# A fused attention and gated-MLP kernel: batch 1's first block set ahead of batch 0's token mixing, token weights and attention 2 placed elsewhere, and k loaded without zeros

## The chip, the cores and the metric

The kernel runs on one core of a Trainium2 chip. Its time is the device time of one execution in microseconds (us), the median of several runs. Before the change it is 541.98 us (three runs, 540.46 to 542.31). The core's engines are TensorE (PE, matmuls, with PEld for its weight loads), VectorE (DVE), ScalarE (ACT), GpSimd (POOL) and SyncE (SP, which here only issues DMA transfers). Each takes its instructions in the order in which the program lists them.

## The reference

There are four batches of 576 positions. A masked attention of 8 heads comes first, then a gated MLP that mixes positions, then a second block that mixes positions again:

```python
scores = where(mask, q @ k.T / sqrt(64), -1e9)   # heads 0-3: the last 32 keys; heads 4-7: earlier keys, same position mod 32
x = softmax(scores) @ v                          # (4, 576, 512) after the heads are put side by side
h = relu(x @ w_in); u, v = h[..., :512], h[..., 512:]
v_n = (v - mean(v)) / sqrt(var(v) + 1e-6)
x = (u * (w_spatial @ v_n + b_spatial)) @ w_out
theta = x @ w_theta
y = w_tok_r @ (x * cos(theta)) + w_tok_i @ (x * sin(theta))
z = x + y
out = z + relu(z @ w_ch)
```

## The kernel before

Nearly all matmuls use pairs of 16-bit numbers (a high part and the rest) with three passes for each product, so each operand is split once by ACT (high part) and by DVE or POOL (low part). The weights arrive as 64-bit words and are converted on the way: a part of a weight is loaded into a staging buffer, `from_f64` (L196) makes 32-bit numbers of it with one ACT and three DVE instructions, and `part` (L209) splits it with one ACT and one POOL instruction. The token weights `wtok` (for `w_tok_r` and `w_tok_i`) come in nine such parts, `wch` (for `w_ch`) in four.

For each batch b the PE's main work goes through these steps, named here as in the trace: **v** (`main_v`: x times the half of `w_in` that is normalized; its result `vn` comes from DVE, ACT and POOL), **u** and **sp** (`main_mid`: the other half of `w_in`, and the first mixing of positions, which reads `vn`; the order is u0, u1, u2, sp0, u3, sp1, sp2, sp3), **x** (times `w_out`), **th** (times `w_theta`, after which cosine and sine and two DMA transposes per quarter fill `zz`), **y** (the token mixing, which reads `zz` and `wtok`) and **c** (times `w_ch`, and out). The steps of one batch follow each other, except that v of the next batch stands between th and y: v covers the time in which `zz` is filled.

Attention runs beside that. It has eleven units (two blocks of two heads) per batch. Batches 0 and 1 use 32-bit numbers (`attention32`), batches 2 and 3 pairs of 16-bit ones (`attention`). A unit is: scores on PE, maximum and exponential, division by the sum (`softmax_div`), a transpose, the product with v, and `x_evac`, which writes the result to `xT` of its batch on ACT and DVE. In `attention32` the mask is added by PE (a matmul with an identity, L383), and the maximum is a DVE reduction (L395). Its k is laid out with zeros, so that one product of 128 rows serves one head of a pair: half of each k load is zeros from memory.

The order of the side work is set by a clock that counts the columns of the main matmuls (`clock`, in us at 2400 columns per us): attention b does a step when the clock passes `ATT_AT[b]` (first step, distance), and a weight part is put in when the clock passes its due time less a lead less a distance for each part after it (`CONV_...`: due, lead, distance). The five constants and the main loop are:

```python
ATT_AT = (None, (2.7, 4.0), (74.5, 4.4), (169.9, 4.6))
CONV_TOK = (61.0, 10.0, 2.0)
...
for b in range(B):
    run_main(main_mid(b))
    end = main_end(b)
    if b + 1 < B:
        drain(b + 1)
        run_main(main_v(b + 1))
    run_main(end)
```

`main_mid` holds u, sp, x and th here, `main_end` y and c. A scheduler then orders each engine's instructions by priority and by its own estimate of when operands are ready.

Of the kernel before, what the change touches and what calls it, by code (L numbers as in the profile page):

```python
# [19 lines left out]
STRIDE = 32  # L20
# [14 lines left out]
E_WAY = ('aaaadaaadaa', 'aaaaaaaaaaa')  # L35
# [18 lines left out]
ATT_AT = (None, (2.7, 4.0), (74.5, 4.4), (169.9, 4.6))  # L54
WIN_AT = (0, 0, 0, 0, 1, 1, 1, 1)
# [3 lines left out]
CONV_TOK = (61.0, 10.0, 2.0)  # L59
CONV_CH = (87.0, 14.1, 2.4)  # L60
# [4 lines left out]
def kernel(  # L65
# [68 lines left out]
    nc.gpsimd.tensor_copy(identb, ident)  # L134
# [166 lines left out]

    def load32(b, hp):
        local = hp < 2
        nb = 6 if local else 5
        qv = att_p.tile([P, S], F32, tag="qT", name="q32", bufs=2)
        kv = att_p.tile([P, 2, S + STRIDE], F32, tag="kT", name="k32", bufs=2)
        ksrc = kzl[b, hp] if local else kzs[b, hp - 2]
        first = b == 0 and hp == 0
        cuts = (0, 2 * LQ, S) if first else (0, S)
        for i, (c0, c1) in enumerate(zip(cuts, cuts[1:])):  # L310
            nc.sync.dma_start(qv[:, c0:c1], qp[b, hp][:, c0:c1])
            k0, k1 = (c0 + STRIDE if i else 0, c1 + STRIDE) if local else (c0, c1)
            nc.sync.dma_start(kv[..., k0:k1], ksrc[..., k0:k1])
            if first and i == 0:
                nc.sync.dma_start(mask, mask_d)
                nc.scalar.activation(maskb, mask, AF.Copy)
        vv = att_p.tile([P, 6, 2, 64], F32, tag="vT", name="v32", bufs=2)
# [21 lines left out]

# [35 lines left out]
    def scores32(u, tabs, sc, apart):  # L375


        R = LQ if units[u][0][0] < 2 else P
        mi = [mask_of(*un) for un in units[u]]
        for j0, j1 in ((0, 1), (1, 2)) if apart else ((0, 2),):  # L380
            for i0, i1 in [(0, 2)] if mi[0] == mi[1] else [(0, 1), (1, 2)]:
                shape = [P, i1 - i0, j1 - j0, P]
                nc.tensor.matmul(sc[0:R, i0:i1, j0:j1], identb[:, 0:R],  # L383
                                 maskb[:, mi[i0], :].unsqueeze(1).unsqueeze(1).broadcast_to(shape),
                                 start=(i0 == 0), stop=False)
        for n, (hp, j, blk) in enumerate(blocks_of(u)):
            o = LQ * blk if hp < 2 else SOFF[blk]
            nc.tensor.matmul(sc[0:R, n // 2, j], tabs[hp][0][:, o:o + R], tabs[hp][1][:, j, o:o + P],
                             start=False, stop=(n == 3 or (apart and n == 2)))
        return R  # L390

    def softmax32(sc, sm, st, R, way):
        X = mybir.AxisListType.X
        mx = st[0:R, 0, :]
        nc.vector.tensor_reduce(out=mx.rearrange("p (i j) -> p i j", i=2), in_=sc[0:R], op=ALU.max, axis=X)  # L395
        smv = sm[0:R].rearrange("p (i j) k -> p i j k", i=2)
        if way == "d":
            nc.vector.tensor_tensor(smv, sc[0:R], mx.rearrange("p (i j) -> p i j", i=2).unsqueeze(3).broadcast_to(
                [R, 2, 2, P]), ALU.subtract)
            nc.scalar.activation(sm[0:R], sm[0:R], AF.Exp, scale=0.125)  # L400
            nc.vector.tensor_reduce(out=st[0:R, 2, :], in_=sm[0:R], op=ALU.add, axis=X)
        else:
            nc.vector.tensor_scalar(st[0:R, 1, :], mx, -0.125, None, op0=ALU.mult)
            for n in range(4):
                nc.scalar.activation(sm[0:R, n, :], sc[0:R, n // 2, n % 2, :], AF.Exp, bias=st[0:R, 1, n:n + 1],
# [488 lines left out]
```

## Time and profile before

| what | us |
|---|---|
| median of three runs | 541.98 |
| the profiled execution's own time | 538.83 |
| its span in the trace | 536.8 |
| PE busy in the span | 485.4 |
| DVE busy | 366.2 |
| ACT busy | 306.9 |
| POOL busy | 96.1 |

The span is the stretch that the trace shows; 2.03 us of the profiled execution lie around it. A row of a timeline begins with start and duration in us, then engine, line of the kernel, operation and operands (out<-in), then shape and count, and in brackets the idle time just before and what ended it. A row of a group has after its bar the busy time in us, the mean duration of one in ns, and the idle time before them with its releasers.

### The profile page before, as it was taken

Reading aid. Unit: us, or ns where it says so; the run is one execution under the profiler, and the core shown is the slowest. Engines: PE = TensorE matmul, PEld = TensorE weight load, DVE = VectorE, ACT = ScalarE, POOL = GpSimd, SP = SyncE. Lnnn points to the kernel's source line nnn. Section 1 sums busy time; section 2 is a strip of 40 time slices with the busy share of each in tenths; the row PEclk is TensorE's granted clock in tenths of the full one; section 3 lists DMA queues with packets and bytes.
Section 4 is the critical chain, followed back from the end, with each engine's and each line's share of the span. In section 5 each row is a group of like instructions: output and inputs, shape, how many; then the busy total and the mean of one; then the engine's idle time right before and its main releaser. Section 6 shows DMA issues by size and latency. Waiting matters only on the chain. (4 is left out here: it accounts for less than half of the span.)

```text
span 536.8 us, 10338 instructions
## 1 busy us (share of the span) xinstructions
PE 485.4 (90%) x4019; PEld 365.7 (68%) x4019; DVE 366.2 (68%) x817; ACT 306.9 (57%) x737; POOL 96.1 (18%) x72
## 2 busy tenths in 40 slices
PE   6777978777887998999899998999999999996996
PEld 6764556555653776777666876777747777774775
DVE  1788999999987998898558778874389121227212
ACT  1777787667798436777585457764582121158101
POOL 0021134543300542001000400010003300100110
PEclk9789999999898998999999999999999999998999
DMA  8666577454159514755529034522082020004402
GB/s 278 239 232 189 162 262 219 161 152 139 37 98 244 136 40 108 194 135 143 137 40 137 1 81 127 148 45 37 1 150 27 1 89 1 1 2 91 86 1 88
DMA packets 75861, 59.88 MB, mean 112 GB/s; under 512 B 59939, under 2 KB 60963, under 8 KB 75813
## 3 DMA queue, kind: packets, MB, share of 16 engines
q1 hardware_dynamic: 75812, 59.23, 42.2%
q8 instruction: 31, 0.51, 0.4%
q14 instruction: 18, 0.14, 0.1%
HBM read 40.08 MB, written 4.72 MB: 83 GB/s over the span
## 5 line engine op out<-in xcount | busy, mean ns | idle before, releaser
L517 PE MATMUL y<-wtok,zf 128*128 128x288 f16 x864 | 108.8, 288 | 4.1 <-DMA zf<-vn 4.1
L517 PEld LDWEIGHTS <-zf 128*128 128x128 f16 x864 | 84.6, 99 | 27.7 <-DMA zf<-vn 4.7
L517 PE MATMUL sp<-wsp,vn 128*128 128x288 f16 x384 | 50.8, 286 | 2.1 <-ACT vn L108 1.6
L517 PE MATMUL c<-x2h,wch 128*128 128x288 f16 x384 | 49.6, 289 | 1.6 <-ACT o L108 1.6
L517 PE MATMUL x<-zf,wout 128*128 128x288 f16 x384 | 49.7, 288 | 0.0
L517 PE MATMUL th<-x2h,wth 128*128 128x288 f16 x384 | 49.6, 290 | 0.0
L517 PE MATMUL u<-xT,win 128*128 128x288 f16 x384 | 49.5, 286 | 0.0
L517 PEld LDWEIGHTS <-vn 128*128 128x128 f16 x416 | 40.3, 98 | 12.3 <-ACT vn L108 1.8
L578 PE MATMUL v<-win,xT 128*128 128x512 f16 x192 | 44.9, 387 | 3.0 <-DVE xT L356 1.9
L108 POOL TENSOR_TENSOR x2h<-x2f,x2h 128x576 f16<-128x576 f32 x20 | 27.6, 1381 | 110.4 <-DVE x2h L108 42.5
L517 PEld LDWEIGHTS <-wch 128*128 128x128 f16 x384 | 37.8, 99 | 11.7 <-issue 2.0
L517 PEld LDWEIGHTS <-wth 128*128 128x128 f16 x384 | 38.1, 100 | 10.3 <-issue 0.2
L517 PEld LDWEIGHTS <-wout 128*128 128x128 f16 x384 | 37.2, 98 | 9.5
L517 PEld LDWEIGHTS <-win 128*128 128x128 f16 x384 | 37.2, 98 | 9.1
L336 ACT ACTIVATE sm<-sm,st 96x128 f32<-96x128 f32 (+1 forms) x88 | 34.2, 390 | 7.8 <-DVE st L332 7.7
L578 PEld LDWEIGHTS <-xT 128*128 128x128 f16 x192 | 18.8, 99 | 25.3 <-DVE xT L356 2.6
L108 ACT ACTIVATE x2h<-x2f 128x576 f16<-128x576 f32 x24 | 16.5, 686 | 30.4 <-DVE x2f L108 30.0
L108 DVE SCALAR_TENSOR_TENSOR x2f<-y,x2f 128x576 f32<-128x576 f32 x16 | 12.0, 752 | 28.5 <-PE y L517 28.5
L108 POOL TENSOR_TENSOR zf<-u,zf 128x576 f16<-128x576 f32 x8 | 10.3, 1287 | 106.5 <-ACT zf L108 106.5
L108 DVE TENSOR_TENSOR ta<-ta,x2f 128x1152 f32<-128x1152 f32 x16 | 21.5, 1352 | 8.9 <-ACT ta L108 8.9
L108 ACT ACTIVATE o<-c 128x576 f32<-128x576 f32 (+1 forms) x17 | 10.3, 613 | 30.3 <-PE c L517 30.0
L343 DVE TENSOR_TENSOR sm<-sm,st 96x512 f32<-96x512 f32 (+1 forms) x33 | 26.7, 809 | 0.8
(122 smaller groups left out, 890.2 us busy)
## 6 DMA issues: line engine op xcount, KB each, us to landing
qs<-in_qd_dram SPq DMA_DIRECT2D x16, 288.0 KB, 3.0
out_dram<-o SPq DMA_DIRECT2D x15, 288.0 KB, 2.1
x2f<-in_w_in_dram SPq DMA_DIRECT2D x8, 512.0 KB, 5.3
ks<-in_kl_dram SPq DMA_DIRECT2D x8, 304.0 KB, 3.1
k<-in_kzs_dram SPq DMA_DIRECT2D x4, 576.0 KB, 5.4
wstg<-in_w_tr_dram SPq DMA_DIRECT2D x4, 576.0 KB, 4.7
wstg<-in_w_ti_dram SPq DMA_DIRECT2D x4, 576.0 KB, 4.7
ks<-in_ks_dram SPq DMA_DIRECT2D x8, 288.0 KB, 3.2
```

The costliest lines, as they stand in the source:

```text
L108: return f(*args, **kwargs)
L336: nc.scalar.activation(sm[0:R, n, :], sm[0:R, n, :], AF.Exp, bias=st[0:R, 1, n:n + 1], scale=-1.0, accum_out=st[0:R, 2, n:n + 1])
L343: N[eng].tensor_tensor(sm[0:R], sm[0:R], st[0:R, 3, :].unsqueeze(2).broadcast_to([R, 4, P]), ALU.mult)
L517: nc.tensor.matmul(ps, lhs, rhs, **kw)
L578: nc.tensor.matmul(ps, xh[:, xe, c, i * P:(i + 1) * P], win[:, we, c, DM:2 * DM], start=(c == 0 and n == 0), stop=(c == NC - 1 and n == 2))
```

## The change

1. The main loop: `main_mid` is cut in two (`main_mid` with u, sp, x, and `main_th` with th). Batch 1's v, u, sp and x now stand ahead of batch 0's y and c; batch 1's th follows c. From v of batch 2 on the order is that of before.
2. Since batch 1's x is made while batch 0's is still needed, batch 1 uses memory that is free then: its gated product lies in `wch`'s place (`gs`), x in that of `xT[0]` and of `vn`, its z in that of `x2h`. Batch 2's attention writes `xT[1]`, batch 3's `xT[0]` (`XAT`).
3. Times of the side work: the nine token parts go from clock 35 to 51 to clock 48.8 to 80, `wch` from 65.7 to 72.9 to 112.5 to 123, attention 2 starts at 63.0 with steps of 5.6 (74.5 with 4.4), attention 3 at 188.5 with 4.0 (169.9 with 4.6). Parts of `w_in` go in from step 3 of attention 0 on, seven of them by step 9 (four by step 7).
4. Attention 0 and 1 are separate functions. In attention 0 the mask is added and the maximum taken in one DVE instruction per block (`softmax_exp`, four per unit), as in attention 2; PE adds no mask there. Its division is on POOL (`softmax_div("g", ...)`, it was "v"); one unit also subtracts on POOL (way "p").
5. k of batches 0 and 1 lies in two fixed tiles, `kts`, whose zero halves are written once by four DVE memsets; each load brings the two non-zero quarters as two DMAs of 64 partitions. The first k loads are issued by ACT.

```diff
-ATT_AT = (None, (2.7, 4.0), (74.5, 4.4), (169.9, 4.6))
-WIN_AT = (0, 0, 0, 0, 1, 1, 1, 1)
+ATT_AT = (None, (2.7, 4.0), (63.0, 5.6), (188.5, 4.0))
+WIN_AT = (0, 0, 0, 1, 1, 1, 1, 1, 1, 1)
...
-CONV_TOK = (61.0, 10.0, 2.0)
-CONV_CH = (87.0, 14.1, 2.4)
+CONV_TOK = (107.0, 27.0, 3.9)
+CONV_CH = (133.0, 10.0, 3.5)
...
+    for t in kts:
+        nc.vector.memset(t[0:64, 1, :], 0.0)
+        nc.vector.memset(t[64:P, 0, :], 0.0)
...
+    gs = [wchf[:, i * S:(i + 1) * S] for i in range(7)] + [gx]
+    x2f1 = xT[0].rearrange("p e c n -> p (e c n)").bitcast(F32).rearrange("p (c n) -> p c n", c=NC)
...
+    XAT = (0, 1, 1, 0)
...
+    def load_kq(qv, kv, b, hp, c0, c1, k0, k1, by=nc.sync):
+        nc.sync.dma_start(qv[:, c0:c1], qp[b, hp][:, c0:c1])
+        ksrc = kzl[b, hp] if hp < 2 else kzs[b, hp - 2]
+        for j in range(2):
+            by.dma_start(kv[64 * j:64 * j + 64, j, k0:k1], ksrc[64 * j:64 * j + 64, j, k0:k1])
...
+                for n, (hp, j, blk) in enumerate(blocks_of(s)):
+                    o = LQ * blk if local else SOFF[blk]
+                    nc.tensor.matmul(scs[n][0:R], tabs[hp][0][:, o:o + R], tabs[hp][1][:, j, o:o + P],
+                                     start=True, stop=True)
+                st = att_p.tile([P, 4, 4], F32, tag="st", name="st", bufs=4)
+                softmax_exp(s, scs, sm, st, E_SUM[s])
...
+                softmax_div("g", sm, st, R, XS)
...
     run_main(main_v(0))
-    for b in range(B):
-        run_main(main_mid(b))
-        end = main_end(b)
+    run_main(main_mid(0))
+    run_main(main_th(0))
+    drain(1)
+    run_main(main_v(1))
+    run_main(main_mid(1))
+    run_main(main_end(0))
+    for b in range(1, B):
+        if b > 1:
+            run_main(main_mid(b))
+        run_main(main_th(b))
         if b + 1 < B:
             drain(b + 1)
             run_main(main_v(b + 1))
-        run_main(end)
+        run_main(main_end(b))
```

**First place: ACT at the start of attention 0.** Before, the first conversion of `w_in` (L203, in `from_f64`) stands ahead of the first exponentials (L405):

```order
1 L316 ACT_TABLE_LOAD
2 L316 ACTIVATE maskb<-mask 128x512
3 L203 ACTIVATE x2f<-x2f 128x512
4 L405 ACTIVATE smx,st<-at,st 96x128 x8
5 L119 ACTIVATE win<-x2h 128x512
```

Now the exponentials are L378 and the conversion is L232; L479 copies a transpose, L420 writes `xT`:

```order
3 L119 ACT_TABLE_LOAD
4 L119 ACTIVATE maskb<-mask 128x512
5 L378 ACTIVATE smx,st<-smx,st 96x128 x9
6 L479 ACTIVATE smx<-sc 128x4x96
7 L378 ACTIVATE smx,st<-smx,st 96x128 x2
8 L420 ACTIVATE xT_101<-av 128x192
9 L378 ACTIVATE smx,st<-smx,st 96x128
10 L479 ACTIVATE smx<-sc 128x4x96
11 L232 ACTIVATE x2f<-x2f 128x512
```

The conversion has gone behind twelve exponentials (three units).

**Second place: PE where v of batch 1 ends.** Before, y of batch 0 follows it (v_1744 is batch 1's last piece of v):

```order
1224 L517 LDWEIGHTS xT_96
1225 L517 MATMUL v_1744<-win,xT_96 64x512
1226 L517 LDWEIGHTS xT_96
1227 L517 MATMUL v_1744<-win,xT_96 64x512
1228 L517 LDWEIGHTS zf
1229 L517 MATMUL y_1800<-wtok,zf 128x288
```

Now u of batch 1 follows:

```order
1150 L587 LDWEIGHTS xT_102
1151 L587 MATMUL v_1716<-win,xT_102 64x512
1152 L587 LDWEIGHTS xT_102
1153 L587 MATMUL v_1716<-win,xT_102 64x512
1154 L587 LDWEIGHTS win
1155 L587 MATMUL u_1763<-xT_102,win 128x288
```

and after u0, u1 and u2 (72 matmuls), 16 score matmuls and 12 of the product with v of attention 2, the first use of batch 1's `vn`, with u3 behind it:

```order
1353 L551 MATMUL av<-pT,areg 64x96
1354 L587 LDWEIGHTS vn
1355 L587 MATMUL sp_1888<-wsp,vn 128x288
1356 L587 LDWEIGHTS vn
1357 L587 MATMUL sp_1888<-wsp,vn 128x288
1358 L587 LDWEIGHTS win
1359 L587 MATMUL u_1963<-xT_102,win 128x288
```

Between v and sp of batch 1 stood y and c of batch 0 and three u; now three u stand there.

**Third place: the token parts on DVE.** Before, after the last gated product of batch 0 (u_967 with sp's result, then zf), token parts (L204, L205, L206 on `wx`) are mixed with attention 1 (st, sc):

```order
204 L108 TENSOR_TENSOR zf<-u_967,zf 128x576
205 L395 TENSOR_REDUCE st<-sc 128x4
206 L204 TENSOR_SCALAR wx<-wstg 128x576
207 L403 TENSOR_SCALAR st<-st 128x4
208 L204 TENSOR_SCALAR wx<-wstg 128x576
209 L205 SCALAR_TENSOR_TENSOR wx<-wstg,wx 128x576 x2
210 L206 SCALAR_TENSOR_TENSOR wx<-wstg,wx 128x576 x2
```

At the same place there is now attention 2's first k (L319) in their stead:

```order
260 L108 TENSOR_TENSOR zf<-u_970,zf 128x576
261 L398 TENSOR_REDUCE st<-sc 128x4
262 L319 TENSOR_TENSOR kt_78<-areg,kt_78 128x608
263 L400 TENSOR_SCALAR st<-st 128x4
264 L406 TENSOR_SCALAR st<-st 128x4
```

One token part (of nine) still stands ahead of the end of th of batch 0; the other eight begin after its first cosine and sine work (ta):

```order
297 L108 SCALAR_TENSOR_TENSOR ta_1482<-th_1413,ta_1482 128x576
298 L108 SCALAR_TENSOR_TENSOR ta_1508<-th_1414,ta_1508 128x576
299 L233 TENSOR_SCALAR wx<-wstg 128x576
300 L108 TENSOR_TENSOR ta_1482<-ta_1482,x2f 128x1152
301 L108 SCALAR_TENSOR_TENSOR ta_1544<-th_1519,ta_1544 128x576
302 L108 TENSOR_TENSOR vn<-ta_1482,vn 128x1152
303 L108 TENSOR_TENSOR ta_1508<-ta_1508,x2f 128x1152
304 L234 SCALAR_TENSOR_TENSOR wx<-wstg,wx 128x576
```

Eight parts have moved from ahead of th's evacuation to behind it; two q and two k preparations of attention 2 have moved the other way.

## Rows read from the trace of the kernel before

**Rows 1.** Busy time of each engine in seven stretches: length, then busy us (instructions) of PE, PEld, DVE, ACT, POOL, then the granted TensorE clock, the DMA engines' share and GB/s. The cuts are: the first conversion of `w_in` begins on ACT and DVE (14.1), the first statistics of v of batch 0 begin (59.5), the first cosine and sine work of batch 0 begins on DVE (146.6), v of batch 1 ends (173.4), c of batch 0 begins (201.9), the first cosine and sine work of batch 1 begins on DVE (271).

```profile
0.00:14.10 14.10, 8.73 (x44) 8.26 (x45) 1.60 (x6) 1.91 (x2) 0.99 (x7) 1.00 0.82 277
14.10:59.50 45.40, 36.63 (x273) 26.36 (x273) 38.74 (x98) 34.24 (x123) 9.10 (x7) 0.89 0.67 220
59.50:146.60 87.10, 70.17 (x575) 52.98 (x572) 84.55 (x160) 63.67 (x167) 33.96 (x23) 0.98 0.50 157
146.60:173.40 26.80, 22.02 (x141) 11.88 (x141) 21.62 (x44) 24.98 (x48) 1.28 (x1) 0.94 0.79 165
173.40:201.90 28.50, 27.89 (x246) 22.39 (x246) 27.42 (x60) 12.15 (x20) 13.76 (x9) 1.00 0.34 96
201.90:271.00 69.10, 64.99 (x629) 50.80 (x628) 53.73 (x148) 47.33 (x135) 6.31 (x5) 0.98 0.56 139
271.00:536.80 265.80, 255.02 (x2124) 193.03 (x2122) 138.56 (x305) 122.64 (x248) 30.71 (x22) 0.99 0.28 58
```

**Rows 2.** The timelines of ACT, of DVE and of PE in the first 62 us, around the first exponentials; the last row is the warm-up, six matmuls of the identity.

```profile
14.12 0.67 ACT L203 ACTIVATE x2f<-x2f 128x512 f32<-128x512 f32 x1 [8.14 <-DMA x2f<-in_w_in_dram]
14.72 0.36 ACT L405 ACTIVATE smx<-at,st 96x128 f32<-96x128 f32 x1
...
1.08 0.48 DVE L149 MEMSET k<- 64x512 f16 x1
...
8.42 0.69 DVE L395 TENSOR_REDUCE st<-at 96x4 f32<-96x512 f32 x1 [6.54 <-PE at L388]
14.12 0.43 DVE L204 TENSOR_SCALAR x2h<-x2f 128x512 int32<-128x512 int32 x1 [5.02 <-DMA x2f<-in_w_in_dram]
...
1.36 2.93 PE L794 MATMUL av<-ident 128*128 128x128 f32 x12 [1.36 <-POOL ident masks.py:199]
```

**Rows 3.** Groups of instructions by line and shape, whole span: the parts of an attention unit on DVE (the reduction; the division; in attention 2 and 3 the masked maximum and the read of its accumulator), POOL's split of a token part and of a `w_in` part, and one shape of the mask matmuls of attention 0 on PE.

```profile
L395 DVE TENSOR_REDUCE st<-at 96x4 f32<-96x512 f32 x6 | 4.1, 684 | 8.7 <-PE at L388 8.7
L343 DVE TENSOR_TENSOR smx<-smx,st 96x512 f32<-96x512 f32 x6 | 4.5, 751 | 0.0
L332 DVE CUSTOM_DVE_ANT_0 sm<-sc,mask 96x128 f32<-96x128 f32 x48 | 11.1, 280 | 0.0
L332 DVE DVE_READ_ACCUMULATOR2_ANT st<- 96x1 f32 x48 | 3.8, 78 | 0.0
L211 POOL TENSOR_TENSOR wtok<-wx,wtok 128x576 f16<-128x576 f32 x9 | 13.6, 1520 | 23.2 <-ACT wtok L119 16.7 <-DVE x2h L108 6.5
L211 POOL TENSOR_TENSOR win<-x2h,win 128x512 f16<-128x512 f32 x8 | 10.3, 1296 | 48.7 <-ACT win L119 48.7
...
L383 PE MATMUL at<-maskb,identb 128*128 128x256 bf16 x10 | 2.3, 301 | 0.8 <-ACT smx L405 0.8
```

**Rows 4.** Durations in ns (least, median, greatest) of two lines of DVE, then the timeline of DVE and of POOL around one of the long ones.

```profile
L332 DVE CUSTOM_DVE_ANT_0 sm<-sc,mask x88: 271/282/292, 159.4 to 361.7; 96x128 f32<-96x128 f32 x48, 128x128 f32<-128x128 f32 x40
...
L341 DVE TENSOR_SCALAR st<-st x44: 134/167/2099, 16.4 to 363.0; 96x4 f32<-96x4 f32 x24, 128x4 f32<-128x4 f32 x20
...
80.57 2.10 DVE L341 TENSOR_SCALAR st<-st 96x4 f32<-96x4 f32 x1
...
78.10 4.54 POOL L108 TENSOR_TENSOR vn<-vr,vn 128x1024 f16<-128x1024 f32 x1 [1.65 <-ACT vn L108]
```

**Rows 5.** Groups of DVE in the stretch 59.5 to 146.6: the nine token parts, and attention 2's q and k.

```profile
L206 DVE SCALAR_TENSOR_TENSOR wx<-wstg,wx 128x576 int32<-128x576 int32 x9 | 7.7, 865 | 0.0
L205 DVE SCALAR_TENSOR_TENSOR wx<-wstg,wx 128x576 int32<-128x576 int32 x9 | 7.6, 852 | 0.0
...
L204 DVE TENSOR_SCALAR wx<-wstg 128x576 int32<-128x576 int32 x9 | 5.0, 565 | 1.1 <-POOL wtok L211 1.1
...
L288 DVE TENSOR_TENSOR qT<-qs,qT 64x576 f16<-64x576 f32 x2 | 2.6, 1284 | 0.1
...
L290 DVE TENSOR_TENSOR kT<-ks,kT 128x608 f16<-128x608 f32 x2 | 1.6, 784 | 0.0
```

**Rows 6.** What PE waited for in the stretch 59.5 to 146.6: us in total, times, longest. L445 is attention 1's transpose.

```profile
PE av L445 <- DVE xT L356: 7.7, 5, 3.1
PE av L445 <- DVE sm L343: 5.9, 3, 2.5
PE sp L517 <- ACT vn L108: 1.6, 1, 1.6
```

**Rows 7.** Timelines of PE, DVE and POOL: the end of v and the making of `vn`, of batch 1 (first three rows) and of batch 2 (next three); then the scores of one unit of attention 2 and one u of batch 1.

```profile
172.62 0.83 PE L517 MATMUL v<-win,xT 128*64 128x512 f16 x5
...
193.26 1.94 DVE L108 TENSOR_TENSOR vn<-vr,vn 64x512 f16<-64x512 f32 x2
...
194.29 2.90 POOL L108 TENSOR_TENSOR vn<-vr,vn 128x1024 f16<-128x1024 f32 x1 [1.25 <-ACT vn L108]
...
287.12 1.49 PE L517 MATMUL v<-win,xT 128*64 128x512 f16 x12
...
300.35 1.22 DVE L108 TENSOR_TENSOR vn<-vr,vn 128x1024 f16<-128x1024 f32 x1
...
300.35 3.20 POOL L108 TENSOR_TENSOR vn<-vr,vn 128x1024 f16<-128x1024 f32 x1 [1.25 <-ACT vn L108]
...
223.03 0.62 PE L458 MATMUL sc<-kT,qT 128*128 128x128 f16 x8
223.49 3.10 PE L517 MATMUL u<-xT,win 128*128 128x288 f16 x24
```

More of the change, by code (lines that the diff above doesn't have):

```diff
@@ L310, in load32 @@
         for i, (c0, c1) in enumerate(zip(cuts, cuts[1:])):
-            nc.sync.dma_start(qv[:, c0:c1], qp[b, hp][:, c0:c1])
             k0, k1 = (c0 + STRIDE if i else 0, c1 + STRIDE) if local else (c0, c1)
[L313 to L317, printed above, removed]
+            load_kq(qv, kv, b, hp, c0, c1, k0, k1, nc.scalar if first else nc.sync)
+            if first:
+                nc.sync.dma_start(mask[:, 2 * i:2 * i + 2], mask_d[:, 2 * i:2 * i + 2])
+        nb = 6 if local else 5
         nc.sync.dma_start(vv[:, 0:nb], vl_d[b, hp] if local else vs_d[b, hp - 2])
@@ new lines, in softmax_exp @@
+        if way == "p":
+            nc.gpsimd.tensor_tensor(sm[0:R], sm[0:R], st[0:R, 0, :].unsqueeze(2).broadcast_to([R, 4, P]), ALU.subtract)
+            nc.scalar.activation(sm[0:R], sm[0:R], AF.Exp, scale=0.125)
+            nc.vector.tensor_reduce(out=st[0:R, 2, :], in_=sm[0:R], op=ALU.add, axis=mybir.AxisListType.X)
+        else:
+            for n in range(4):
+                nc.scalar.activation(sm[0:R, n, :], sm[0:R, n, :], AF.Exp, bias=st[0:R, 1, n:n + 1],
+                                     scale=-1.0, accum_out=st[0:R, 2, n:n + 1])
@@ new lines, in softmax_exp, with scores32 @@
+        return R
+    def scores32(u, tabs, sc):
+        R = LQ if units[u][0][0] < 2 else P
+        mi = [mask_of(*un) for un in units[u]]
+        for i0, i1 in [(0, 2)] if mi[0] == mi[1] else [(0, 1), (1, 2)]:
+            nc.tensor.matmul(sc[0:R, i0:i1], identb[:, 0:R],
+                             maskb[:, mi[i0], :].unsqueeze(1).unsqueeze(1).broadcast_to([P, i1 - i0, 2, P]),
+                             start=(i0 == 0), stop=False)
+        for n, (hp, j, blk) in enumerate(blocks_of(u)):
+            o = LQ * blk if hp < 2 else SOFF[blk]
+            nc.tensor.matmul(sc[0:R, n // 2, j], tabs[hp][0][:, o:o + R], tabs[hp][1][:, j, o:o + P],
+                             start=False, stop=(n == 3))
+        return R
@@ L373, in spans_of @@
         return spans
[L375 to L405, printed above, removed]
-                                     scale=0.125, accum_out=st[0:R, 2, n:n + 1])
@@ L411, in attention32, with attention1 @@
+    def attention1():
+        b = 1
+        tabs = {0: load32(b, 0)}
+        copy(N, "v", identb, ident)
+        copy(N, "a", maskb, mask)
         yield
@@ L763 @@
     timed(sq_parts(wch, w_ch), *CONV_CH)
-    atts = [(attention32 if b < N32 else attention)(b) for b in range(B)]
+    atts = [attention0(), attention1()] + [attention(b) for b in range(N32, B)]
     att = {"b": 1, "n": 0}
```

148 lines of the change are left out of this document (100 added, 48 removed).

## The prediction, made before the changed kernel ran

> **What bounds the kernel now.** I read the busy time by stretch first [rows 1]. In the last stretch, from 271 us on, PE is busy 255.0 of 265.8 us: there PE alone decides, and the change leaves the order of that work as it is. Half the span is therefore outside the change. In the first 271 us three stages behave differently. Up to 14.1 us hardly anything but transfers runs (DVE busy 1.6 us). From 59.5 to 146.6 us, which is u, sp, x and the beginning of th of batch 0, DVE is busy 84.55 of 87.1 us and PE 70.17: DVE is the bound. From 146.6 to 271 us PE is busy 22.02 + 27.89 + 64.99 = 114.9 of 124.4 us and DVE 21.62 + 27.42 + 53.73 = 102.8: PE is nearly the bound, with 9.5 us of gaps.
>
> Then the waits of PE in the stage where DVE is the bound [rows 6]: 7.7 and 5.9 us for DVE's last step of a unit of attention 1 or its division. DVE comes late because other work, the weight parts above all [rows 5], stands ahead in its queue.
>
> Last the start [rows 2]. DVE has the first maximum at 8.42 + 0.69 = 9.11 us, but the first exponential (L405) begins at 14.72: ACT sat for 8.14 us in front of a conversion of `w_in` whose transfer had not landed, and the exponentials are queued behind it.
>
> **The change, part by part.** The sum is made against the profiled execution, 538.83 us (span 536.8 and 2.03 around it); the median of the runs shown is 541.98, which is 3.15 more.
>
> *The start, up to 59.5 us.* The conversion now stands behind twelve exponentials on ACT and likewise further down on DVE. So the wait from 9.11 to 14.72 goes: 5.6 us. What is late next is the chain of the unit itself, in which three things change. The reduction (0.684) and the division (0.751) leave DVE, four masked maxima (4 x 0.280, or 4 x 0.358 if the read of the accumulator counts in full) come [rows 3]: per unit between 0 and 0.3 us less, for eleven units 0 to 3.5 us less. The division goes to POOL, where a `w_in` split of nearly the same size takes 1.296 [rows 3]. POOL is free (9.1 of 45.4 us busy, rows 1), but a long POOL instruction can hold up DVE: a DVE tensor_scalar of 0.167 us (median) took 2.10 us, from 80.57 to 82.67, while POOL ran from 78.10 to 82.64 [rows 4]. Eleven divisions cost DVE between nothing and 11 x 1.3 = 14 us that way. The masked maximum is not hit so in the rows (292 ns at most, rows 4), and most of the unit's DVE time is masked maxima now, so I take a fifth of it, 3 us. Four memsets come ahead of the first maximum; a memset of 64x512 16-bit numbers took 0.48 [rows 2], these have 608 32-bit numbers, so 0.5 to 1.2 us each, 2 to 4.6 us in all. They run while the first q, k and mask are still on the way, and the first maximum began only at 8.42, so I take nothing; without that cover up to 4.6 would be lost. The mask matmuls that go (ten of 301 ns are shown, rows 3) and the warm-up, now behind the first scores (2.93 us, rows 2), lie on PE, which idles 8.8 of 45.4 us there; I count both at nothing, and 2.9 us if the warm-up is in the way of the first transposes. Half of k's bytes go; with DMA at 0.67 of its time [rows 1] that can only bring `w_in` sooner, and I count it at nothing too. Together: -5.6 + 3 = -2.6, call it -3, with ends of -9 (no hold-up, all of the DVE saving) and +9 (all 14 us of it).
>
> [...]
>
> *From 59.5 to 146.6 us.* Eight of nine token parts leave it. On DVE a part is 0.865 + 0.852 + 0.565 = 2.28 us [rows 5], some 0.2 less back to back, so 8 x 2.07 = 16.6 us go. Two q and two k of attention 2 come, at the means of other such instructions 2 x 1.284 + 2 x 0.784 = 4.1 [rows 5], of which the q's mean holds a hold-up, so 3.4. DVE's 84.55 becomes 71.4. PE keeps its 70.17. POOL loses eight splits of 1.520 [rows 3], 12.2 of its 33.96 us, and with them some hold-ups. Two engines at 70 to 71 us that wait for each other in order need more than either; with 4 us for that the stage takes 75 us: -12. It cannot go under PE's 70.2, so -17 is one end; the other is -4, where only a part of the 13.6 us of waits [rows 6] shrinks because a unit of attention stays slow for its own latency.
>
> *From 146.6 to 271 us, in its new order.* The token parts land here. PE's work is the same 114.9 us, DVE's rises from 102.8 by 13 to 116 of 124.4 us. By itself that fits. What doesn't is the first use of `vn` of batch 1 in sp0. After v ends at 173.45, DVE's last `vn` is done at 195.20 and POOL's at 197.19: 21.8 and 23.7 us [rows 7]. Before, y and c of batch 0 and three u lay in between and nobody waited. Now PE has three u (3.0 us each from start to start), two groups of scores (0.46) and a product with v: 10.4 us. For batch 2, where DVE has less to do, the same way takes from 288.61 to 301.57 on DVE and 303.55 on POOL, 13.0 and 14.9 us. So PE waits in front of sp0 for between 13.0 - 10.4 = 2.6 and 23.7 - 10.4 = 13.3 us, with u3, sp and x queued behind it. DVE has token parts in that place, so I take 9, nearer to batch 1's row. Behind the wait DVE has caught up, and of the 9.5 us of gaps of before 2 go: +7. The ends are -2 (2.6, and half of the gaps go) and +16 (13.3, and DVE's 116 us late by 3 more at c).
>
> *From 271 us on* the order is the same. Attention 3 is spread over 16 steps of 4.0 instead of 4.6 and begins later; PE is busy 96% there and DVE 52% [rows 1], so nothing, give or take 2.
>
> Sum: -3 - 12 + 7 = -8. 538.83 - 8 = 530.8 for a profiled execution, and 541.98 - 8 = 534.0 for the median, which I predict.
>
> **The rivals.**
> 1. *The wait in front of sp0 is near batch 2's row.* With 2.6 instead of 9 us the last stage costs 0 or so, and the middle one gives 15 as DVE is freer: 541.98 - 3 - 15 = 524. For it speaks that much of DVE's work between v and `vn` in batch 1 was attention 2 and `wch`, which are placed elsewhere now; against it the five token parts that take their place.
> 2. *The middle stage is bound by attention 1's own latency.* Then it gives 4: 541.98 - 3 - 4 + 7 = 542, no change. For it: PE waits for attention units there [rows 6]. Against it: the waits name DVE instructions that stood behind conversions.
> 3. *The other side: the token parts burden the wrong stage.* The place is sp0 of batch 1, the mechanism DVE's queue: the parts stand between v's statistics and `vn`, and their splits on POOL (8 x 1.52 us) hold DVE up as at 80.57 us. The wait is then the full 13.3, half of the 12.2 us of splits is added, and the start gives nothing: -12 + 13.3 + 6 = +7.5, 549.5. It decides once the third stage costs more than the 15 us that the first two give. For it: 21.8 us in batch 1 under load. Against it: the parts are spread over 3.9 us of clock each, twice the distance of before.
> 4. *The divisions on POOL hold DVE up each time.* The start then loses 11 x 1.3 - 5.6 = 8.7 less 1.7 of the DVE saving, +7: 541.98 + 7 - 12 + 7 = 544.
>
> **How the numbers follow.** Forecast 0.45, with a range of its own from 528 to 539; rival 1 0.19; rival 2 0.15; rival 3 0.14; rival 4 0.07. A change under 0.3% (1.6 us) is about what a measurement of this kernel cannot tell from none. Faster: 0.43 of the forecast, 0.19 of rival 1, 0.06 of rival 2 and 0.01 of rival 4, 0.69. Same: 0.02 + 0.05 + 0.02 = 0.09, the rest, 0.22, slower. The range of 8 in 10 takes in rival 1 and rival 2 and half of the way to rival 3: 522 to 546.
>
> **What would show it right or wrong.** The start: ACT's first exponential at some 9 us or sooner, v of batch 0 done about 3 us earlier; DVE instructions of 1 us and more in the first 50 us, where 0.2 or 0.7 is usual, would be the POOL hold-ups. The middle: DVE no longer at 97% from v of batch 0 to the cosine and sine of batch 0, that way 75 us long, PE waiting less for attention 1. The third: PE idle in front of the first sp of batch 1, released by `vn`, 9 us long; no wait of y for `wtok`. From v of batch 2 to the end nothing different. The prediction is wrong if the way from v to sp of batch 1 stalls PE over 15 us, if the middle stage shrinks by less than 6, or if the start comes out longer than before.

## The result, and the profile after

The changed kernel takes 545.49 us (median of 19 runs) against 541.98 before: the ratio is 1.0055, 95% interval 1.0031 to 1.0078. It is slower by half a per cent. The prediction was 534.0, faster; 545.49 lies at the slow end of its widest range (522 to 546).

The profiled execution took 545.56 us, with a span of 543.8. That of before had 538.83 and 536.8, 3.15 under its own median, so of the 7.0 us between the two spans about half belongs to that lucky execution; stages are compared with this in mind.

The busy time by stretch, first of before, then of after. The cuts are the same five events in both, all read from PE: the end of v of batch 0, the start of v of batch 1, the start of th of batch 1, the start of c of batch 1, the end of v of batch 3. Columns as in [rows 1].

```profile
0.00:61.60 61.60, 47.46 (x329) 35.34 (x330) 42.44 (x107) 38.07 (x126) 11.33 (x15) 0.92 0.70 233
61.60:153.20 91.60, 74.57 (x617) 57.29 (x617) 86.82 (x164) 68.33 (x176) 34.00 (x22) 0.98 0.49 152
153.20:264.90 111.70, 102.30 (x905) 75.16 (x904) 97.10 (x242) 75.89 (x186) 20.07 (x13) 0.97 0.59 141
264.90:317.30 52.40, 52.40 (x419) 37.86 (x416) 36.98 (x84) 31.89 (x61) 7.69 (x5) 1.00 0.36 59
317.30:400.60 83.30, 81.15 (x736) 59.53 (x735) 56.30 (x151) 55.66 (x137) 5.11 (x4) 1.00 0.39 86
400.60:536.80 136.20, 127.57 (x1026) 100.53 (x1024) 46.60 (x73) 37.08 (x55) 17.90 (x13) 0.99 0.18 41
```

```profile
0.00:63.10 63.10, 46.92 (x303) 32.17 (x304) 48.64 (x171) 43.07 (x137) 25.45 (x26) 0.92 0.69 211
63.10:146.10 83.00, 74.55 (x624) 58.05 (x625) 67.55 (x140) 58.77 (x161) 22.41 (x14) 0.98 0.38 116
146.10:266.20 120.10, 103.96 (x885) 75.42 (x884) 104.42 (x257) 82.09 (x196) 30.33 (x21) 0.94 0.59 144
266.20:316.90 50.70, 50.70 (x387) 36.05 (x385) 31.49 (x53) 25.61 (x35) 7.63 (x5) 1.00 0.37 80
316.90:406.60 89.70, 85.95 (x779) 62.44 (x777) 63.40 (x184) 62.09 (x164) 5.11 (x4) 0.98 0.43 89
406.60:543.80 137.20, 128.88 (x1024) 101.06 (x1024) 45.09 (x74) 36.85 (x55) 17.78 (x13) 0.97 0.15 38
```

Read down the first number of each row. The start is 1.5 us longer, the middle stage 8.6 shorter, the third 8.4 longer, the fourth and fifth together 4.7 longer (135.7 to 140.4), the last 1.0. At the forecast's own cuts (the events named at [rows 1]) the first three read 0.7 longer, 8.2 shorter and 9.4 longer. In the middle stage PE's busy time is the same to 0.02 us, and its idle time halves from 17.0 to 8.5. In the third stage DVE's busy time grows by 7.3. In the fifth PE idles 3.75 instead of 2.15 us and is busy longer: attention 3 begins later, so more of it falls there (43 instructions), and the matmuls around the new waits are slower.

That last point in the trace. After, PE's timeline in x of batch 2, and the busy time of three stretches there:

```profile
361.64 2.37 PE L587 MATMUL x<-zf,wout 128*128 128x288 f16 x18
365.09 0.52 PE L551 MATMUL av<-pT,areg 128*64 128x126 f16 x12 [1.08 <-DVE xT L421]
366.72 0.61 PE L528 MATMUL sc<-kt,qT 128*128 128x128 f16 x8 [1.11 <-DVE st L369]
367.17 8.45 PE L587 MATMUL x<-zf,wout 128*128 128x288 f16 x54
```

```profile
364.00:368.00 4.00, 1.81 (x26) 1.54 (x26) 3.85 (x15) 3.37 (x13) 0.00 (x0) 0.91 0.41 81
368.00:372.00 4.00, 4.00 (x23) 2.77 (x22) 3.18 (x14) 2.19 (x10) 0.00 (x0) 0.66 0.14 28
372.00:376.00 4.00, 4.00 (x43) 3.01 (x40) 2.27 (x4) 3.29 (x6) 0.00 (x0) 1.00 0.20 37
```

PE waits 2.2 us for two units of attention 3, which come one behind the other. Then the granted clock is 0.66 over 4 us (0.50 from 368 to 370 us), and PE gets 23 instructions done where the next 4 us hold 43. The 54 matmuls from 367.17 take 8.45 us; at the pace of the first row (18 in 2.37) they would take about 7. In this execution the slow matmuls add more than half of the waits' own length.

That is not so each time. u3_first, a kernel described below with the same pacing of attention 3, has the same two waits at the same place:

```profile
365.98 0.52 PE L551 MATMUL av<-pT,areg 128*64 128x126 f16 x12 [1.08 <-DVE xT L421]
367.61 0.61 PE L528 MATMUL sc<-kt,qT 128*128 128x128 f16 x8 [1.11 <-DVE st L369]
368.05 6.78 PE L587 MATMUL x<-zf,wout 128*128 128x288 f16 x54
```

```profile
368.00:372.00 4.00, 4.00 (x37) 3.21 (x35) 3.21 (x15) 2.80 (x13) 0.00 (x0) 1.00 0.05 9
```

The granted clock stays at 1.00, and the 54 matmuls take 6.78 us. Of the seven traces with this pacing, in four (after, before_pace, div_dve, tok_late) the 54 matmuls behind these waits take 7.91 to 8.45 us, in the other three 6.78.

The start, after: the first exponential, what PE waited for up to 62 us, and the groups of DVE and POOL up to 52 us (last two columns: busy us, mean ns).

```profile
7.80 0.39 ACT L378 ACTIVATE smx<-smx,st 96x128 f32<-96x128 f32 x1
```

```profile
PE sc L478 <- POOL smx L408: 8.9, 6, 3.2
PE at L468 <- DMA kt<-in_kzl_dram: 4.4, 2, 3.3
```

```profile
L369 DVE CUSTOM_DVE_ANT_0 smx<-at,mask 96x128 f32<-96x128 f32 (+1 forms) x40 | 9.8, 277 | 6.7 <-PE at L468 6.5
L235 DVE SCALAR_TENSOR_TENSOR x2h<-x2f,x2h 128x512 int32<-128x512 int32 x8 | 9.5, 1191 | 0.0
L234 DVE SCALAR_TENSOR_TENSOR x2h<-x2f,x2h 128x512 int32<-128x512 int32 x8 | 8.4, 1049 | 0.9 <-ACT x2f L232 0.8
L233 DVE TENSOR_SCALAR x2h<-x2f 128x512 int32<-128x512 int32 x8 | 4.7, 585 | 0.0
...
L408 POOL TENSOR_TENSOR smx<-smx,st 96x512 f32<-96x512 f32 (+1 forms) x11 | 13.6, 1242 | 19.5 <-DVE st L406 11.1 <-DVE st L407 3.6 <-ACT x2f L232 2.6
```

The first exponential stands at 7.80 instead of 14.72 [rows 2]: that part worked. But the conversions of `w_in` (L233 to L235) are stretched. Before, up to 52 us, the same three lines took:

```profile
L206 DVE SCALAR_TENSOR_TENSOR x2h<-x2f,x2h 128x512 int32<-128x512 int32 x6 | 4.1, 680 | 0.0
L205 DVE SCALAR_TENSOR_TENSOR x2h<-x2f,x2h 128x512 int32<-128x512 int32 x6 | 4.1, 675 | 0.6 <-ACT x2f L203 0.6
L204 DVE TENSOR_SCALAR x2h<-x2f 128x512 int32<-128x512 int32 x7 | 2.9, 420 | 5.7 <-DMA x2f<-in_w_in_dram 5.7
```

Eight parts at 420 + 675 + 680 ns make 14.2 us; after they took 22.6, 8.4 more. And PE waits 8.9 us for divisions on POOL. The lead of 7 us is spent that way by the end of v.

### The profile page after: what moved, and what is told of

Read it like the earlier page. It is cut to its first block, busy times and chain, and to the rows that moved or that the text cites. A ratio compares the mean times of both kernels' runs of the same rounds, so it can differ in the third digit from the quotient of the medians.

```text
span 543.8 us, 10391 instructions
## 1 busy us (share of the span) xinstructions
PE 491.0 (90%) x3993; PEld 365.2 (67%) x3993; DVE 360.6 (66%) x876; ACT 308.5 (57%) x744; POOL 108.7 (20%) x83
## 5 line engine op out<-in xcount | busy, mean ns | idle before, releaser
L587 PE MATMUL y<-wtok,zf 128*128 128x288 f16 x864 | 110.4, 290 | 3.9 <-DMA zf<-vn 3.9
L587 PE MATMUL sp<-wsp,vn 128*128 128x288 f16 x384 | 52.8, 293 | 3.4 <-ACT vn L108 2.4
L587 PE MATMUL c<-x2h,wch 128*128 128x288 f16 x384 | 48.8, 286 | 0.7 <-ACT o L108 0.7
L378 ACT ACTIVATE sm<-sm,st 96x128 f32<-96x128 f32 (+1 forms) x88 | 34.1, 389 | 18.3 <-DVE st L369 17.9
L108 POOL TENSOR_TENSOR x2h<-x2f,x2h 128x576 f16<-128x576 f32 x15 | 20.1, 1339 | 115.2 <-ACT x2h L108 60.9
L587 PE MATMUL x<-zf,wout 128*128 128x288 f16 x288 | 38.3, 294 | 0.0
L587 PE MATMUL th<-x2h,wth 128*128 128x288 f16 x288 | 36.8, 286 | 0.0
L108 DVE SCALAR_TENSOR_TENSOR x2f<-y,x2f 128x576 f32<-128x576 f32 x12 | 9.0, 754 | 31.1 <-PE y L587 31.0
L108 ACT ACTIVATE x2h<-x2f 128x576 f16<-128x576 f32 x18 | 12.3, 684 | 27.7 <-DVE x2f L108 27.6
L108 DVE TENSOR_TENSOR u<-u,sp 128x576 f32<-128x576 f32 x16 | 12.0, 748 | 20.8 <-PE sp L587 20.8
L408 DVE TENSOR_TENSOR sm<-sm,st 96x512 f32<-96x512 f32 (+1 forms) x33 | 24.5, 743 | 0.8
L369 DVE CUSTOM_DVE_ANT_0 sm<-sc,mask 96x128 f32<-96x128 f32 (+1 forms) x88 | 21.1, 281 | 4.3 <-PE sc L528 4.3
```

What stands on the lines that cost most here:

```text
L108: return f(*args, **kwargs)
L408: N[eng].tensor_tensor(sm[0:R], sm[0:R], st[0:R, 3, :].unsqueeze(2).broadcast_to([R, 4, P]), ALU.mult)
L587: nc.tensor.matmul(ps, lhs, rhs, **kw)
```

## The experiments

Every ratio is to the kernel before, run beside it (its median there lay between 540.9 and 541.6 us). Stage lengths are from the profiled executions with the cuts used above. Stages whose code is the same in several kernels show how far one execution differs from another: the changed start, up to the end of v of batch 0, took 62.6 to 65.1 us in twelve kernels; the middle and third stage together took 200.8 to 204.0 us in the five that differ in attention 3 alone (after, pace3, xswap, swap_dense, swap_late). And a profiled execution can lie off its kernel's median: those of div_dve and swap_dense 3.9 and 2.0 us under it, those of pace3, xswap and tok_before 3.6, 2.9 and 2.5 over it.

### Attention 3's pacing

**pace3**: the changed kernel with `ATT_AT[3]` back.

```
-ATT_AT = (None, (2.7, 4.0), (63.0, 5.6), (188.5, 4.0))
+ATT_AT = (None, (2.7, 4.0), (63.0, 5.6), (169.9, 4.6))
```

> The changed kernel with attention 3 begun and spread as before (169.9, 4.6). Between c of batch 1 (317 us) and the end of v of batch 3 the changed kernel loses 6.4 us on the kernel before. Theory A (the denser, later pacing of attention 3 makes the loss: PE waits 3.6 us for its maxima and for xT, and PE works at a clock of 0.93 in between): most of the loss goes, v of batch 3 ends 3 to 5 us earlier than 406.5, no wait of v for xT, and the time is 541 to 543 us. Rival B (the same attention work merely stands later, and the units wait wherever they stand): c of batch 1 ends later by what v of batch 3 wins, and the time is 545 us, within 1.

Measured: 540.37 us, 0.9999 (0.9963 to 1.0035). Fourth and fifth stage 52.9 + 83.2 = 136.1 us, 4.3 less than after. Here attention 3 writes over x of batch 1 before c of batch 1 has added it, for `x2f1` lies in `xT[0]`; so this version only measures time. It also shows why a later start is in the change: the new buffers force it.

**xswap**: the same pacing, made free of that reuse.

```
+    xT3 = x2f.rearrange("p c n -> p (c n)").bitcast(F16).rearrange("p (e c n) -> p e c n", e=2, c=NC)
-    XAT = (0, 1, 1, 0)
+    XAT = (0, 1, 1, 2)
+    xT = xT + [xT3]
...
-        return x2f1 if b == 1 else x2f
+        return x2f if b == 0 else x2f1
```

> The changed kernel with attention 3 paced as before (169.9, 4.6), made free of the reuse that forces the late start: in the changed kernel attention 3 writes its rows into the memory that holds x of batch 1 until c of batch 1. Here it writes them into the memory of x of batch 0, and batches 2 and 3 keep x where batch 1 had it; the instructions and their order are else those of pace3. Theory A (the time of pace3 comes from the pacing alone): 539 to 542 us, v of batch 3 ends 83 to 84 us after c of batch 1 begins (89.7 in the changed kernel). Rival B (the early writes disturb something else, or pace3's time came from its spoilt x): 544 to 547 us.

Measured: 540.51 us, 0.997 (0.9941 to 0.9999). By the time theory A. By the trace not quite: v of batch 3 ends 85.1 us after c of batch 1 begins, not 83 to 84, and the fourth and fifth stage take 138.0 us, 2.4 less than after. This kernel has a wait of its own in c of batch 1, and the matmuls behind it are slow: 48 take 7.71 us, where the 36 ahead of it took 4.57, and the mean of c's matmuls is 310 ns (286 in the changed kernel):

```profile
PE av L553 <- DVE x2f L423: 2.0, 1, 2.0
```

swap_tok and swap_tok_u3 below have the same pacing and memory without that wait, and take 135.6 and 135.9 us there.

**before_pace**: the kernel before, with the change's `(188.5, 4.0)` alone.

> The kernel before with only attention 3's pacing of the change (188.5, 4.0). Theory A (the pacing alone costs some 5 us wherever it stands): 545 to 548 us, v of batch 3 ends 88 to 91 us after c of batch 1 begins (83.3 in the kernel before), with waits of PE for maxima and xT and a lower clock there. Rival B (it costs only in the changed kernel's order): 541 to 543 us.

Measured: 547.52 us, 1.0115 (1.0081 to 1.0149). Fourth and fifth stage 50.1 + 91.0 = 141.1 us against 135.7, with the waits of after and one pair more, and x of batch 2 slow in the same way. PE's waits from 318 us, and the group of x (a mean of 286 ns in the kernel before):

```profile
PE av L481 <- DVE xT L356: 1.8, 2, 1.1
PE sc L458 <- DVE st L332: 1.8, 3, 1.1
PE v L578 <- ACT xT L355: 0.9, 1, 0.9
```

```profile
L517 PE MATMUL x<-zf,wout 128*128 128x288 f16 x96 | 13.9, 310 | 0.0
```

So the pacing costs 5.0 us by the medians (4.6 by the ratios) when taken out of the changed kernel and 5.9 when put into the kernel before: as far as the intervals tell, it doesn't depend on the new order.

**swap_dense** and **swap_late**: xswap with `(169.9, 4.0)`, early but dense, and with `(180.0, 4.6)`, late but no denser than before.

> xswap with attention 3 begun at its place of before but with the change's step (169.9, 4.0). It tells which of the two numbers costs the time. Theory A (density: units 4.0 us apart come faster than their maxima and exponentials): 543 to 546 us, with waits of PE for maxima again. Rival B (lateness: the last units meet x and th of batch 2, whose own evacuations stand on DVE and ACT, and end just ahead of v of batch 3): 539 to 541 us, as xswap, no waits of PE for maxima from 317 us on.

> xswap with attention 3's step of before (4.6) but begun so late (180.0) that its last step falls at 253.6 on the planner's clock, as in the changed kernel (252.5 by 188.5 + 16 x 4.0; 243.5 in xswap). Theory A (the late end costs: the last units meet x and th of batch 2 and the start of v of batch 3): v of batch 3 ends 139 to 141 us after th of batch 1 begins (138.0 in xswap, 140.4 in the changed kernel), PE waits there for maxima and xT, and the time is 543 to 546 us. Rival B (the dense steps cost): 137 to 138.5 us in the trace and 539 to 541.5 us.

Measured: dense 543.1 us, 1.0051 (1.0015 to 1.0087); late 541.01 us, 0.9988 (0.9956 to 1.002). With xswap (540.51) and after (545.49) that is a table of two by two: density costs 2.6 us early and 4.5 late, lateness 0.5 and 2.4 (by the ratios 4.4 and 3.6, and 1.0 and 0.2). Density is the larger part, as far as intervals of about 1.8 us to either side allow. The corner of after has the change's own memory; pace3 and xswap, 540.37 and 540.51, show no cost of that. swap_late's two stages take 135.9 us, as rival B had it. In swap_late PE has none of the waits inside x any more, only the last one, at v:

```profile
PE v L650 <- ACT x2f L422: 0.9, 1, 0.9
PE v L650 <- DVE x2f L423: 0.2, 1, 0.2
```

One thing doesn't fit: swap_dense's profiled execution has 138.3 us in the two stages, as xswap's (138.0), with the same two waits and no new ones, so by the trace it is rival B. But that execution was its fastest, at 541.11, and xswap's its slowest, at 543.44: these traces cannot show where its 2.6 us go. That density costs is shown by waits for the late start alone.

### The start

**div_dve**: the divisions of batch 0 on DVE again, no subtraction on POOL.

```
-E_SUM = 'aaaaaaaapaa'
+E_SUM = 'aaaaaaaaaaa'
...
-                softmax_div("g", sm, st, R, XS)
+                softmax_div("v", sm, st, R, XS)
```

> The changed kernel with batch 0's divisions on DVE instead of POOL and no unit with the subtraction on POOL. In the changed kernel's trace the 24 DVE instructions of the w_in conversions take 22.6 us up to 52 us, where the kernel before's durations (0.420, 0.675, 0.680 us) give 14.2: 8.4 us of stretching, and PE waits 8.9 us for divisions on POOL. Theory A (POOL holds DVE up, rival 4 of the prediction): the three conversion steps fall back to 0.42, 0.68, 0.68 us, v of batch 0 ends at 58 to 61 us instead of 63.0, and the time is 541 to 543 us. Rival B (DVE is full either way: eleven divisions of 0.8 us come back, 8.9 us, as much as the stretching): the conversions are short again but v of batch 0 ends at 62 to 64 us and the time stays at 545 us, within 1.

Measured: 546.92 us, 1.0093 (1.0055 to 1.013): no gain. Up to 52 us:

```profile
L408 DVE TENSOR_TENSOR smx<-smx,st 96x512 f32<-96x512 f32 (+1 forms) x11 | 8.3, 757 | 0.1
L234 DVE SCALAR_TENSOR_TENSOR x2h<-x2f,x2h 128x512 int32<-128x512 int32 x8 | 7.7, 965 | 0.2 <-ACT x2f L232 0.2
L235 DVE SCALAR_TENSOR_TENSOR x2h<-x2f,x2h 128x512 int32<-128x512 int32 x8 | 5.4, 680 | 0.0
L233 DVE TENSOR_SCALAR x2h<-x2f 128x512 int32<-128x512 int32 x8 | 3.8, 478 | 1.2 <-DMA x2f<-in_w_in_dram 1.2
```

L235 is back at 680 ns: the divisions on POOL did stretch it. L234 is not, at 965: three of its eight run beside POOL's splits of `w_in` and take 1215 to 1652 ns, the five that run beside nothing on POOL 677 to 693. The conversions take 16.9 us, 5.7 less, and the divisions bring 8.3. v of batch 0 ends at 60.7, as theory A had it, but v of batch 1 begins at 145.9, where after has 146.1, though this execution was the kernel's fastest. The time is rival B's or worse.

**start_before**: batch 0's whole softmax as before (mask by matmul, maximum and division on DVE, `WIN_AT` as before) in the changed kernel.

> The changed kernel with the softmax of batch 0's attention as before: the mask put in by matmuls, one maximum for four blocks, exponentials from PSUM (two units with the subtraction on DVE), the division on DVE, the w_in parts at their places of before. Theory A (the new softmax and its divisions on POOL lose the 6 us that the earlier first unit wins): v of batch 0 ends at 60 to 62 us instead of 63 to 64.6, and the time is 542 to 544 us. Rival B (v of batch 1 begins at 146 to 147 us whenever v of batch 0 ends, as it did with the divisions on DVE): the middle stage takes back what the start wins, and the time is 545 us, within 1.

Measured: 548.03 us, 1.0117 (1.0077 to 1.0157). v of batch 0 ends at 60.7, the middle stage takes 87.8, together 148.5; with the changed start, and the token parts where the change puts them, the same way took 146.1 to 148.0 in six kernels. So the later end of v of batch 0 seems to be no loss: the changed start is worth 0.5 to 2.4 us at the start of v of batch 1 (against a single trace of start_before), 2.5 us in the medians, though the two intervals touch. Neither theory was right: the time is 3 us over rival B's.

### The token parts and the wait in front of sp0

**tok_before** and **tok_late**: the changed kernel with the parts beside batch 0's u, sp and x as before, and behind sp0 of batch 1.

```
-CONV_TOK = (107.0, 27.0, 3.9)
+CONV_TOK = (61.0, 10.0, 2.0)    # tok_before
+CONV_TOK = (107.0, 3.0, 3.0)    # tok_late
```

> The changed kernel with the token parts back at the planner's places of before (61, 10, 2): beside u, sp and x of batch 0. Theory A (the parts only carry the same DVE time from one stage to another): the way from the end of v to the end of th of batch 0 grows from 83 to 90 to 93 us, the way from v of batch 1 to th of batch 1 shrinks from 120.1 to 110 to 113, and the time is 545 us, within 1.5. Rival B (the move is a true gain, as the prediction had it): the first grows by 8 and the second shrinks by 3 or less, and the time is 549 to 552 us. Rival C (the move is the fault): the second shrinks by more than the first grows, and the time is 541 to 543 us.

> The changed kernel with the token weights' nine parts put between sp0 of batch 1 and y of batch 0 on the planner's clock (lead 3, gap 3) instead of around v of batch 1. Theory A (the parts hold the scratch buffers and DVE between v and vn of batch 1): the way from the end of v to sp0 of batch 1 falls from 20.7 to 13 to 16 us, the middle stage (end of v of batch 0 to end of th of batch 0) shortens by 1 to 3, and the time is 539 to 542 us if mid of batch 1 takes the parts in its gaps. Rival B (the parts cost the same wherever they stand: DVE is filled from v of batch 1 to y of batch 0): what sp0 wins is lost in x of batch 1 or in a wait of y for wtok, and the time is 544 to 548 us.

Measured: tok_before 542.73 us, 1.0029 (1.0007 to 1.0051), middle 91.8 and third 110.6 us; tok_late 547.77 us, 1.0128 (1.0085 to 1.0171), middle 82.3, third 121.5. In both the parts carry their time along: middle and third together are 202.4 with tok_before, 203.1 after, 203.8 with tok_late, which one execution can't tell apart. tok_before's trace fits its theory A; its median is 2.8 us under that of after (rival C), but by the ratios it is 1.4, and the intervals overlap.

tok_late is the sharper one. The way from the end of v to sp0 of batch 1 fell from 20.6 to 11.4 us, further than expected, and the stage got no shorter. sp0 begins at 171.5 here; the stage cut at 180 and 232 us:

```profile
146.50:180.00 33.50, 30.96 (x227) 19.29 (x226) 27.87 (x69) 25.04 (x47) 3.40 (x2) 1.00 0.73 162
180.00:232.00 52.00, 43.30 (x369) 32.53 (x367) 50.80 (x115) 35.43 (x89) 22.88 (x13) 0.90 0.53 150
232.00:268.00 36.00, 31.94 (x297) 23.84 (x295) 32.66 (x77) 21.38 (x59) 9.88 (x7) 0.95 0.52 131
```

DVE is busy 50.80 of 52 us behind sp0, and PE pays there, at a clock of 0.90.

**u3_first**: the changed kernel with the fourth u of batch 1 ahead of sp0.

```
+            u = x2f1[:, 3, :] if b == 1 and m == 3 else s1(f"u{m}")
...
+        if b == 1:
+            order[3], order[4] = order[4], order[3]
```

> The changed kernel with one edit: the fourth u of batch 1 ahead of the first sp. Theory A (the wait in front of sp0 is idle time of PE that this work fills): the way from v of batch 1 to th of batch 1 shrinks from 120.1 to 117 to 118 us, and the time is 542 to 543.5 us. Rival B (DVE's queue sets that stage's length): 119 to 121 us in the trace, and 545 us, within 1.

Measured: 545.17 us, 1.0065 (1.003 to 1.0101), third stage 118.6. By the time rival B; the trace has half of theory A's gain, within what executions of the same code differ by. Both runs say the same: shortening or filling the wait in front of sp0 gained nothing.

### Together

**all3** is the three first edits at once (pacing as in pace3, with the same overwritten x of batch 1; divisions on DVE; parts late). **swap_tok**, **swap_tok_u3**, **swap_tokmid**, **best_wide** build on xswap: parts as before; the same with u3 first; parts at `(85.0, 10.0, 4.5)`; swap_tok_u3 with attention 3 at `(157.0, 5.3)`.

> The three edits at once: divisions on DVE, attention 3 paced as before, token parts behind sp0 of batch 1. If the three losses are separate (theory A of each), they add: 545.5 - 3.5 - 3.5 - 5 = 533 to 537 us. If DVE is full in the first 200 us either way (rival B of each), only the pacing shows: 541 to 546 us.

> The version of xswap (attention 3 paced as before, its rows in the memory of x of batch 0) with the token parts at their places of before as well. If the two gains against the changed kernel (5.0 us by xswap, 2.8 us by tok_before) are separate, they add: 537 to 539 us, faster than the kernel before by 3 to 5. If the token parts' gain came only with the changed kernel's attention 3, 540 to 542 us.

> swap_tok with the fourth u of batch 1 ahead of the first sp (its result in memory of x of batch 1 that is free until then), so that PE has one block of 3 us more to do while vn of batch 1 is made. Theory A (the wait in front of sp0 is plain idle time of PE, as the prediction costed it): 2 to 3 us less than swap_tok, sp0 of batch 1 still 14 to 15 us behind v. Rival B (PE only waits later, in x or y of that stage, because DVE sets its length): as swap_tok, within 1.

> xswap with the token parts spread over both stages on the planner's clock (85, 10, 4.5: from 39 to 75, half of them beside x and th of batch 0, half beside v and u of batch 1). If PE's and DVE's idle time can be evened out over the two stages, it beats xswap and swap_tok: 536 to 538 us. If the parts cost the same wherever they stand, 540 to 541 us.

> swap_tok_u3 (537.3 us) with attention 3 begun at 157.0 in steps of 5.3, so that it ends at 241.8. If lateness and density both cost, it gains another 1 to 2 us: 535 to 536.5. If the gain is used up once the units no longer meet x of batch 2, 537 us, within 1. If the earlier units meet y and c of batch 1 and attention 2's end instead, 538 to 540 us.

Measured: all3 548.28 us, 1.0133 (1.0078 to 1.0188), a miss: the pacing's gain is not there (139.3 us in the fourth and fifth stage, with 3.8 us of waits of PE for `xT`), and the middle stage takes 86.7, the third 121.9. swap_tok 539.53, 0.9974 (0.994 to 1.0007): the gains of xswap and tok_before don't show added up, for the ratio is xswap's. swap_tok_u3 **537.3, 0.9936 (0.9902 to 0.9969)**: faster than both kernels, with a third stage of 106.1 us; its 2.2 us on swap_tok (third stage 106.4) lie within the intervals, and its trace does not show them. In these two the middle and third stage together take 199.0 and 198.8 us, less than in any kernel that has the parts where the change or tok_late puts them. swap_tokmid 546.55, 1.0124 (1.0072 to 1.0177): spreading the parts is the worst, 87.0 + 123.1 us in the middle and third stage. best_wide 540.7, 0.9973 (0.9932 to 1.0015): no further gain.

## Why the prediction was wrong

*The step that failed: "From 271 us on the order is the same ... so nothing, give or take 2".* It was +5.0, or +5.9 by before_pace. The argument was from shares of a stage, PE 96% and DVE 52% busy [rows 1]. But DVE's work comes in bursts, however idle DVE is on average: from 364 to 368 us of after it is busy 3.85 of 4 us, with the steps of two units, the split of a gated product and a preparation of attention's v in one queue, and PE waits 2.2 us there. swap_late, with steps of 4.6, has DVE at 2.95 in that stretch and no wait. At PE's 96% such waits lengthen the stage, and in four of seven traces the slow matmuls behind them did so again (7.91 to 8.45 us for 54, against 6.78). That two units meet because the chain of one is longer than 4.0 us is not measured. That the buffers force a later start was in the diff and not seen.

*The start, -3.* It was +1.5 at the end of v of batch 0, and start_before suggests that this cut misleads: by v of batch 1 the new start is ahead. The chance of 0.07 for rival 4 was too small: the mechanism was there, 8.4 us of stretching where I took 3 for the hold-ups. Its price was not paid in full, for DVE would have had 8.3 us of divisions instead (div_dve). That its 544 comes near the 545.49 is luck: it has the stretching at full price and nothing for the pacing. (Rival 3's terms add up to 7.3, not 7.5.)

Not every DVE instruction was stretched. L234 and L235, two inputs in SBUF, took a mean of 1049 and 1191 ns instead of 675 and 680; the masked maximum, with one input in PSUM, 277 against 280 [rows 3]. The tensor_scalar L233, with one input, took 1006 and 1172 ns in two of its eight, both beside POOL, and 410 to 429 in the others. What sets these instructions apart, no run shows.

*The middle stage, -12.* It was -8.6. DVE's work fell further than the 13 us worked out (by 19 at these cuts), but PE's 74.55 us of work plus 8.5 of waits remain, where 4 us were allowed for the two engines' mutual waits. What PE waits for is attention 1's own steps:

```profile
PE av L515 <- DVE xT L421: 4.4, 4, 2.5
PE sc L387 <- ACT sm L402: 1.6, 1, 1.6
PE av L515 <- DVE sm L408: 1.5, 1, 1.5
```

That is rival 2 in part. One term of the sum was small: by the rows a token part takes 2.26 us of DVE's busy time ((7.7 + 7.6 + 5.0) / 9, [rows 5]), not 2.07, so eight are 18.0 us, not 16.6.

*The third stage, +7.* It was +8.4, and PE waits between v and sp0, as forecast. PE's and DVE's timelines after:

```profile
163.68 0.83 PE L587 MATMUL v<-win,xT 128*64 128x512 f16 x5
...
170.87 6.04 PE L587 MATMUL u<-xT,win 128*128 128x288 f16 x48 [3.31 <-ACT vr L108]
...
181.06 1.01 PE L528 MATMUL sc<-kt,qT 128*96 128x128 f16 x8 [3.71 <-DVE st L369]
...
185.14 0.66 PE L587 MATMUL sp<-wsp,vn 128*128 128x288 f16 x2 [2.38 <-ACT vn L108]
...
185.21 4.31 DVE L108 TENSOR_TENSOR vn<-vr,vn 128x1024 f16<-128x1024 f32 x2
```

From the end of v (164.5) to sp0 are 20.6 us, in which PE is busy 11.2: 9.4 us of waits, where 9 were forecast. The number was right and the reading not. The forecast had all of it for `vn`; that is the last wait, 2.4 us, and the others are for the evacuation of v (`vr`) and for a maximum of attention 2. And tok_late took most of the wait away and the time stayed. So the sum of the middle and the third stage, -5 as forecast, was -0.2 in the traces: what the middle stage won, the third gave back. It is not the sum of DVE's work that sets the two stages. By the tables that fell from 183.9 to 172.0 us, and PE still idles 24.6 us where it idled 26.4. What the traces show is DVE full in places: in the 20.6 us behind v it is busy 20.3, in tok_late 50.8 of 52 behind sp0. Why 12 us less of DVE work brought nothing is open.

With the pacing taken out (xswap) the rest of the change is worth 1.1 us on before, 0.3% (interval down to 0.0), where -8 was forecast. So of the error of 11.5 us some 5 are the pacing and 6.5 the rest. No run divides the 6.5. In the traces the start was 4.5 us over its term at its cut, and the middle and third stage together 4.8 over theirs, gains counted in the one and given back in the other; if start_before's 2.5 us is the worth of the start, its term was nearly right and the rest lies in those two stages. The new order of the main loop, the places of attention 2 and of `wch`, and the k loads were not run alone, so what each brings is not known.

## What to carry to other kernels

An edit of a pacing table is a term of the sum: look at what else the unit's engines have to do in the few us where its steps will fall, not at their busy shares over the stage. When work moves between stages, forecast the two stages together before counting the gain of one, and don't take a fall in an engine's busy time for a gain: ask which waits of the busiest engine go. And where new buffer sharing comes with a later start, look at whether the start is the price of the sharing: another assignment of the same memory (xswap) gave some 5 us back.

## What the runs showed of the hardware

The same short waits were followed by slow matmuls in one execution and not in another. Behind 2.2 us of waits in 364 to 368 us the granted clock of after was 0.66 over 4 us, and 54 matmuls of x took 8.45 us; behind the same waits u3_first had a clock of 1.00, and the same matmuls took 6.78. What decides it, no run shows.

And DVE instructions differed in how far they were stretched beside POOL. In after the two-input L235 took 676 ns with nothing on POOL beside it and 1170 to 1412 in the other seven; two of the eight one-input L233 took 1006 and 1172 instead of some 420; of the 40 masked maxima in the same 52 us none took more than 292 ns.
